# Moving the far attention's softmax up in the order, and six products of the first group from VectorE to GpSimd, in a fused attention and feed-forward kernel

## The chip, the cores and the metric

The kernel runs on one core of a Trainium2 chip. A core has a matrix engine (TensorE, "PE"; its weight loads are listed as "PEld"), a vector engine (VectorE, "DVE"), a scalar engine (ScalarE, "ACT"), a general engine (GpSimd, "POOL") and a queue that issues most transfers (SyncE, "SP"). Each takes its own instructions strictly in the order laid down when the kernel was compiled; semaphores make one wait for another. The metric is the device time of one execution in microseconds (us).

## The reference

For 8 batches of 8 heads, 576 positions and 64 columns the reference adds two attentions and sends the sum through a feed-forward layer. Cut to what matters:

```python
q_d = q.reshape(B, H, Sd, factor, D).mean(axis=3)      # factor 4, so Sd = 144; k_d, v_d alike
out_up = np.repeat(sm_attn(q_d, k_d, v_d), factor, axis=2)
mask = np.abs(pos[:, None] - pos[None, :]) < factor    # 7 neighbours
out_local = softmax(where(mask, scale * q @ k.T, -1e9)) @ v
x = (out_up + out_local).transpose(0, 2, 1, 3).reshape(B * S, H * D)   # 4608 x 512
h = x @ w_in                                           # 512 x 2048
g = s * np.maximum(h, 0) ** 2 + b
return g @ w_out                                       # 2048 x 512
```

The texts call the first attention **far** (all positions, four to a block) and the second **near** (seven neighbours).

## The kernel before

**Feed-forward.** The 4608 rows are cut into 18 token tiles of 256 (t = 0 to 17), the 2048 inner columns into 8 parts (p = 0 to 7). For each pair (t, p) TensorE forms `ph` (L781) from `xh` and `xl`, the high and the low part of x, and the weights `wi`. ACT takes relu, square and the high part `gh` or `gb` (L796 to L798), VectorE the low part `gl` (L803), and TensorE adds the product with `wo` into `po` (L871 to L873). These matmuls stand on TensorE in an order that the program writes out by hand (`products`, L1037): each is tied behind the one before, and `chain_end` is the last one issued so far. A tile needs `xh` and `xl` of its rows; they are cut from x by a cast on ACT (L758) and a subtraction on VectorE (L759).

**Attention.** A batch has 576 rows, that is two and a quarter tiles. Tile 6 (rows 1536 to 1791) is the first that holds rows of batch 3, tile 9 the first of batch 4. Batches 0 to 2 are worked by a long order written out by hand (`PLAN`). Batches 3 to 7 are worked in 10 **groups** (`GROUPS`, `two_pairs`), two to a batch. A group has two **halves** (of near work) and two **units** (of far work), a unit being one pair of heads of a batch. So there are 20 halves and 20 units; groups 0 and 1 are batch 3 with units 0 to 3, and x of a batch is complete when both of its groups have been added to it.

**Near work of a half** (`two_pairs`, L651). For seven offsets POOL multiplies q by shifted k into `pr` (L673; in the first group every second one is VectorE's), VectorE sums each product over the columns (L675). `pr` has two buffers. Then comes a short softmax on VectorE and ACT (L684 to L692), then seven more offsets in which VectorE multiplies v by a weight (L702) and POOL or VectorE adds to `acc` (L703; in the first group always VectorE). The half's data `lqk` has one buffer, so the next half's load is issued when the last product of this half has been formed. At a group's end VectorE transposes `acc` (L713), SP stores it to DRAM (L718) and loads it back in another layout (L723), and POOL adds it to x (L731), which is issued one half later.

**Far work of a unit** (`far_chain`, L556). It is a generator that `two_pairs` calls at every third offset, five steps to a unit:

1. `begin_far`: VectorE sums q and k in blocks of four (L529, L531), ACT spreads q into `dq` (L535).
2. On TensorE the unit before is ended: `up` from its probabilities in `both` (tile `pd`) and the values in `dq` (L547, L549). Right behind it stand this unit's scores `sa` (L578). ACT spreads `up` over x (L552). Then come VectorE's maximum (L589), ACT's scaling of it (L590) and three exponentials with sums (L592).
3. ACT's sum with the small constant (L596), VectorE's reciprocal (L597), ACT's three scalings (L599).
4. Two transposes on VectorE into `ft` (L606), two stores to DRAM (`away`, L610), and seven loads back into `both` in the layout that `up` needs (L615, L621).
5. Nothing.

`far_values` prepares the unit's values on POOL, issued between steps 2 and 3: `vt` and `vq` (L310, L311), then `dq` (L314, L315), which must wait until the `up` of the unit before has read the old ones. The second transpose writes into the same single buffer as `vt`.

**What sets the order.** The framework lays down each engine's order when it compiles the kernel. Among instructions that can go it prefers the one issued earlier in the program. Inside `tc.high_priority()` an instruction is ranked as if it stood at the program's start, so it is preferred to all that is not. L796 to L803 are issued like this, and so are `up` and `sa`, which besides are tied behind `chain_end` on TensorE (`behind`). Steps 3 and 4 and the maximum and exponentials of step 2 are not.

Of the kernel before, what the change touches and what calls it, by code (L numbers as in the profile page):

```python
# [11 lines left out]
F32 = mybir.dt.float32  # L12
# [34 lines left out]
GQ = 48  # L47
NQ = SD // GQ
# [38 lines left out]
def attention_ffn_kernel(ctx, tc, qk, vw_in, vr_in, vdm, qkn, vn, w_in, w_out, s_in, b_in, out):  # L87
    nc = tc.nc
# [3 lines left out]
    def pool(name, bufs, gap=0):  # L92
        if gap:
            ctx.enter_context(tc.tile_pool(name="gap_" + name, bufs=1)).tile(
                [P, gap // 4], F32, name="gap")
        return ctx.enter_context(tc.tile_pool(name=name, bufs=bufs))
# [6 lines left out]
    one = pool("one", 1)  # L103
# [8 lines left out]
    def bank(i, shape, name):  # L112
        return ps.tile(shape, F32, tag=f"k{i}", name=name)
# [442 lines left out]
    def far_chain(units, banks):  # L556

        held = None
        for b, hp in units:
            kd = begin_far(b, hp)  # L560
            yield
            with tc.high_priority(), behind(nc.tensor.engine, chain_end):
                spread = held and end_far(*held, banks)
                with behind(nc.tensor.engine):
                    scores = far_scores(kd, banks)
            if held:
                spread()
            held = b, hp, (yield from far_rest(b, hp, scores))
            yield
        with behind(nc.tensor.engine, chain_end):  # L570
            spread = end_far(*held, banks)
        spread()

    def far_scores(kd, banks):

        sa = banks([2 * GQ, NQ, SD], "sa")
        for i in range(NQ):
            nc.tensor.matmul(sa[:, i], diag[0][1][:, i], kd, start=True, stop=True)  # L578
        return sa

    def far_rest(b, hp, sa):

        tmp = lambda shape, name, tag: one.tile(shape, F32, tag=tag, name=name)
        n = 2 * GQ
        dmx = tmp([P, 2, NQ], "dmx", "dmx")[0:n]
        both = tmp([P, NQ * SD], "pd", "pd")
        pd = both[0:n].rearrange("p (i k) -> p i k", i=NQ)
        dsm = tmp([P, NQ], "dsm", "dsm")[0:n]
        nc.vector.tensor_reduce(dmx[:, 0], sa, AX.X, ALU.max, negate=True)  # L589
        nc.scalar.mul(dmx[:, 1], dmx[:, 0], SCALE / 16)  # L590
        for i in range(NQ):
            nc.scalar.activation(  # L592
                pd[:, i], sa[:, i], AF.Exp, bias=dmx[:, 1, i : i + 1],
                scale=SCALE / 16, accum_out=dsm[:, i : i + 1])
        yield
        nc.scalar.activation(dsm, dsm, AF.Identity, bias=eps[0:n], scale=4.0)  # L596
        nc.vector.reciprocal(dsm, dsm)  # L597
        for i in range(NQ):
            nc.scalar.mul(pd[:, i], pd[:, i], dsm[:, i : i + 1])  # L599
        yield  # L600


        away = {}
        for k0, w, tag in ((0, 3, "ptm"), (KM, 2, "vt")):
            ft = tmp([n, w, n], "ft", tag)
            nc.vector.transpose(  # L606
                ft.rearrange("p w (h i c) -> p w i h c", h=2, i=NQ),
                pd[:, :, k0 : k0 + 32 * w].rearrange("p i (w h c) -> p w i h c", w=w, h=2))
            away[k0] = far_off.tile([n, w, n], F32, name="away")
            nc.sync.dma_start(away[k0], ft)  # L610
        pm = both[0:KM, 0 : 3 * n].rearrange("p (r n) -> p r n", r=3)
        pr = both[:, 3 * n : 3 * SD].rearrange("p (r n) -> p r n", r=3)
        for w in range(3):
            m = min(32, KM - 32 * w)
            nc.sync.dma_start(  # L615
                pm[32 * w : 32 * w + m],
                away[0][:, w].rearrange("(r a) n -> a r n", r=3)[0:m])
        for h in range(2):
            for w in range(2):
                at = 64 * h + 32 * w  # L620
                nc.sync.dma_start(  # L621
                    pr[at : at + 32],
                    away[KM][:, w, GQ * h : GQ * h + GQ].rearrange("(r a) n -> a r n", r=3))
        yield
        return both

    halves = [(b, g, h) for b, g in GROUPS for h in range(2)]
    near_in = {}
# [13 lines left out]
    def load_far(i, parts):  # L642
        if i < len(far_units):
            load_parts(*far_units[i], parts)
# [6 lines left out]
    def two_pairs(b, g, dn):  # L651

        at = GROUPS.index((b, g))
        i = 0

        def far():
            nonlocal i
            if i % 3 == 2:
                next(dn)
            if i == 17:  # L660
                load_far(2 * at + 2, ("qk",))
            i += 1

        acc = None
        st = bank(7, [P, 2, P], "st")
        for h in range(2):
            half = 2 * at + h
            lqk, lv = near_in[half, "lqk"], near_in[half, "lv"]
            ls = take(st[:, h], 0, [P, CH, NO])
            sums = st[:, h, 64 : 64 + CH]  # L670
            for o in range(NO):
                pr = two.tile([P, CH, D], F32, tag="pl", name="pr")
                (nc.vector if at == 0 and o % 2 else nc.gpsimd).tensor_tensor(  # L673
                    pr, lqk[:, 0:CH], lqk[:, CH + o : 2 * CH + o], ALU.mult)
                nc.vector.tensor_reduce(ls[:, :, o], pr, AX.X, ALU.add)  # L675
                if o == NO - 1:
                    load_near(half + 1, "lqk")
                    far_values(half)
                    while late:
                        late.pop()()  # L680
                far()
                yield
            row = lambda t: t.unsqueeze(2).to_broadcast([P, CH, NO])
            nc.vector.tensor_tensor(ls, ls, omask, ALU.add)  # L684
            lr = two.tile([P, 2, CH], F32, tag="lr", name="lr")
            nc.vector.tensor_reduce(lr[:, 0], ls, AX.X, ALU.max)
            nc.vector.tensor_tensor(ls, ls, row(lr[:, 0]), ALU.subtract)
            nc.scalar.activation(ls, ls, AF.Exp, scale=SCALE)
            nc.vector.tensor_reduce(sums, ls, AX.X, ALU.add)
            nc.vector.tensor_scalar(sums, sums, 1e-9, None, ALU.add)  # L690
            nc.vector.reciprocal(lr[:, 1], sums)
            nc.vector.tensor_tensor(ls, ls, row(lr[:, 1]), ALU.mult)  # L692
            far()
            yield
            acc = acc or two.tile([P, CH, 2, D], F32, tag="qk", name="acc")
            for o in range(NO):
                w = ls[:, :, o : o + 1].to_broadcast([P, CH, D])
                if o == 0:
                    nc.vector.tensor_tensor(acc[:, :, h], lv[:, 0:CH], w, ALU.mult)
                else:  # L700
                    pv = two.tile([P, CH, D], F32, tag="pv", name="pv")
                    nc.vector.tensor_tensor(pv, lv[:, o : o + CH], w, ALU.mult)  # L702
                    (nc.vector if at == 0 or o % 3 == 1 else nc.gpsimd).tensor_tensor(  # L703
                        acc[:, :, h], acc[:, :, h], pv, ALU.add)
                if o == NO - 1:
                    load_near(half + 1, "lv")
                far()
                yield
        x = xt[b]
        moved, away = [], []  # L710
        for h in range(2):
            ft = two.tile([P, 2, CH * 32], F32, tag="pv", name="ft")
            nc.vector.transpose(  # L713
                ft.rearrange("p e (i b) -> p e i b", i=CH),
                acc[:, :, h].rearrange("p i (e a) -> p e i a", e=2))
            moved.append(ft)
            away.append(far_off.tile([P, 2, CH * 32], F32, name="away"))
            nc.sync.dma_start(away[h], ft)  # L718
        load_far(2 * at + 3, ("qk",))
        yield  # L720
        for u in range(2):
            for e in range(4):
                nc.sync.dma_start(  # L723
                    moved[u][32 * e : 32 * e + 32],
                    away[e // 2][64 * u : 64 * u + 64, e % 2].rearrange("(r a) n -> a r n", r=2))
        yield

        def add():
            for u in range(2):
                xv = x[:, 2 * g + u].rearrange("p (r b i) -> p r b i", r=2, b=32)  # L730
                nc.gpsimd.tensor_tensor(  # L731
                    xv, moved[u].rearrange("p r (i b) -> p r b i", i=CH), xv, ALU.add)
            complete.update((b, 2 * g + u) for u in range(2))

        late.append(add)
        yield
# [92 lines left out]
    held = {}  # L829
# [149 lines left out]
    at = {"sa": 0, "tp": 0, "up": 0, "tr": 1, "sl0": 1, "sl1": 0, "ol": 1}  # L979
# [225 lines left out]
```

## Time and profile before

| what | value |
|---|---|
| median of 3 runs | 945.68 us (943.19 to 946.14) |
| the profiled execution, its own time | 947.76 us |
| its span, first to last instruction | 946.0 us |
| mean granted TensorE clock | 0.991 |

The profile is of one execution. Its page gives each engine's busy time; the windows give the same for stretches of time, with the granted clock (third number from the end), the share of the DMA engines and GB/s behind the engines. A line of the timeline has the start and the duration in us, the engine, the source line, the operation, the tiles (out<-in) and in brackets how long the engine idled before it and on whom it waited. A line of the waits has the total in us, the number of times and the longest. "SPq" is SP's queue. Matmuls are pipelined, so their spacing, not their listed length, is what one costs.

### The profile page before, as it was taken

How to read it: one execution, taken by the hardware profiler on the slowest of the kernel's cores; microseconds unless marked ns; L12 is line 12 of the kernel's file. 1: busy time of each engine (PE TensorE's matmuls, PEld its weight loads, DVE VectorE, ACT ScalarE, POOL GpSimd, SP SyncE). 2: the span in 40 equal slices, each digit the busy share in tenths (PEclk: the TensorE clock that was granted, in tenths of full speed). 3: DMA queues.
4: the chain of work that ended last, by engine and by line, in shares of the span. 5: the costliest groups of instructions: out<-in, count | busy, mean ns of one | idle time of the engine just before them, and what ended most of it. 6: DMA issues, size and time to landing. Idle time of an engine off the chain costs nothing.

```text
span 946.0 us, 18560 instructions
## 1 busy us (share of the span) xinstructions
PE 907.2 (96%) x7106; PEld 815.8 (86%) x7106; DVE 665.6 (70%) x1148; ACT 462.2 (49%) x1073; POOL 434.7 (46%) x447
## 2 busy tenths in 40 slices
PE   6699999999999997999999999999989999999998
PEld 5588888788888896999988998899889899999997
DVE  9999999854599888878888778777879662111111
ACT  7977774466464352534444444534344433233331
POOL 6401120010324778777877778787887730000000
PEclk9989999999999998999999999999999999999999
DMA  9755413122343445444343526353444220000000
GB/s 322 270 161 195 147 46 119 46 92 71 112 122 95 152 130 157 135 127 133 113 154 115 155 86 174 95 175 113 122 135 131 74 73 1 23 1 24 1 23 23
DMA packets 60505, 105.09 MB, mean 111 GB/s; under 512 B 20480, under 2 KB 34048, under 8 KB 60416
## 3 DMA queue, kind: packets, MB, share of 16 engines
q1 hardware_dynamic: 56096, 96.03, 32.9%
q10 hardware_dynamic: 4320, 7.87, 2.2%
q8 instruction: 56, 0.92, 0.4%
q14 instruction: 33, 0.27, 0.1%
HBM read 84.85 MB, written 19.02 MB: 110 GB/s over the span
## 4 chain that ended last, share of the span: by engine, by line
PE 30%; POOL 15%; DVE 12%; DMA 8%; SPq 3%; issue 3%; ACT 1%; DVEq 0%; POOLq 0%; ACTq 0%
PE ph L781 15%; POOL pr L673 9%; POOL acc L703 5%; PE po L871 5%; PE po L872 5%; PE po L873 5%; DMA lqk<-in_qkn_dram 4%; DVE pv L702 2%; DVE acc L703 2%; DMA tqk<-in_qk_dram 2%; DVE st L675 2%; DMA pd<-away 1%; SPq L723 1%; DMA away<-ft 1%; SPq L621 1%
## 5 line engine op out<-in xcount | busy, mean ns | idle before, releaser
L781 PE MATMUL ph<-xh,wi 128*128 128x256 f32 x2176 | 412.8, 280 | 6.0 <-ACT xh L758 4.7
L781 PEld LDWEIGHTS ph<-xh,wi 128*128 128x128 f32 x2176 | 345.8, 189 | 15.4 <-ACT xh L758 5.2
L781 PE MATMUL ph<-xl,wi 128*128 128x256 f32 x1152 | 320.6, 278 | 0.0
L673 POOL TENSOR_TENSOR pr<-lqk 128x576 f32<-128x576 f32 x134 | 198.2, 1501 | 80.3 <-DMA lqk<-in_qkn_dram 45.3
L781 PEld LDWEIGHTS ph<-xl,wi 128*128 128x128 f32 x1152 | 217.9, 189 | 7.6
L796 ACT ACTIVATE ph<-ph 128x512 f32<-128x512 f32 x144 | 83.8, 582 | 265.3 <-PE ph L781 256.8
L871 PE MATMUL po<-wo,gh 128*128 128x512 f32 x416 | 165.9, 399 | 0.2 <-DVE os L836 0.2
L872 PE MATMUL po<-wo,gh 128*128 128x512 f32 x416 | 163.6, 393 | 0.0
L873 PE MATMUL po<-wo,gl 128*128 128x512 f32 x416 | 162.9, 392 | 0.7 <-DVE gl L803 0.6
L803 DVE TENSOR_TENSOR gl<-ph,gh 128x512 fp32r<-128x512 f32 x104 | 71.0, 682 | 92.9 <-ACT gh L798 92.6
L675 DVE TENSOR_REDUCE st<-pr 128x9 f32<-128x576 f32 x140 | 105.2, 752 | 43.6 <-POOL pr L673 42.5
L703 POOL TENSOR_TENSOR acc<-acc,pv 128x576 f32<-128x576 f32 x72 | 104.6, 1453 | 46.9 <-DVE acc L703 24.2
L314 POOL TENSOR_TENSOR dq<-vt 80x64 f32<-80x64 f32 x58 | 21.1, 377 | 174.4 <-PE up L385 173.0
L702 DVE TENSOR_TENSOR pv<-lv,st 128x576 f32<-128x576 f32 x120 | 87.3, 745 | 18.5 <-POOL acc L703 18.0
L873 PEld LDWEIGHTS po<-wo,gl 128*128 128x128 f32 x416 | 78.3, 188 | 18.6 <-DVE gl L803 1.5
L871 PEld LDWEIGHTS po<-wo,gh 128*128 128x128 f32 x416 | 78.2, 188 | 13.2 <-ACT pd L599 0.4
L872 PEld LDWEIGHTS po<-wo,gh 128*128 128x128 f32 x416 | 78.5, 189 | 11.3 <-issue 0.2
L797 ACT ACTIVATE ph<-ph 128x512 f32<-128x512 f32 x144 | 83.8, 582 | 3.7
L798 ACT CAST gh<-ph 128x512 fp32r<-128x512 f32 x104 | 61.0, 587 | 20.1 <-PE po L872 16.8
L871 PE MATMUL po<-wo,gb 128*128 128x512 f32 x160 | 62.9, 393 | 0.3 <-DVE os L836 0.3
L872 PE MATMUL po<-wo,gb 128*128 128x512 f32 x160 | 62.8, 392 | 0.0
L873 PE MATMUL po<-wo,gb 128*128 128x512 f32 x160 | 62.4, 390 | 0.0
(176 smaller groups left out, 1200.1 us busy)
## 6 DMA issues: line engine op xcount, KB each, us to landing
tqk<-in_qk_dram SPq DMA_DIRECT2D x30, 584.0 KB, 4.0
lqk<-in_qkn_dram SPq DMA_DIRECT2D x20, 768.0 KB, 4.6
lv<-in_vn_dram SPq DMA_DIRECT2D x20, 480.0 KB, 3.5
out_dram<-os ACTq DMA_DIRECT2D x30, 256.0 KB, 3.2
wst<-in_moe_w_in_dram SPq DMA_DIRECT2D x7, 1024.0 KB, 5.9
wst<-in_moe_w_out_dram SPq DMA_DIRECT2D x7, 1024.0 KB, 5.1
away<-ft SPq DMA_DIRECT2D x20, 288.0 KB, 2.3
ft<-away SPq DMA_DIRECT2D x80, 72.0 KB, 2.0
```

The lines of the kernel that those rows point to most:

```text
L673: (nc.vector if at == 0 and o % 2 else nc.gpsimd).tensor_tensor(pr, lqk[:, 0:CH], lqk[:, CH + o : 2 * CH + o], ALU.mult)
L675: nc.vector.tensor_reduce(ls[:, :, o], pr, AX.X, ALU.add)
L702: nc.vector.tensor_tensor(pv, lv[:, o : o + CH], w, ALU.mult)
L703: (nc.vector if at == 0 or o % 3 == 1 else nc.gpsimd).tensor_tensor(acc[:, :, h], acc[:, :, h], pv, ALU.add)
L781: nc.tensor.matmul(ph[:, j], wi[p][:, s, k, f], xk[:, k], start=k == 0 and s == 0 and xk is xh, stop=k == NK - 1 and s == 1)
L796: nc.scalar.activation(ph, ph, AF.Relu)
L797: nc.scalar.activation(ph, ph, AF.Square)
L798: nc.scalar.copy(gh, ph)
L803: nc.vector.tensor_tensor(gl, acc.pop((t, p)), gh.bitcast(F32), ALU.subtract)
L871: nc.tensor.matmul(po[m], gh[:, j, ms], wo[p][:, 0, j], start=first, stop=False)
L872: nc.tensor.matmul(po[m], gh[:, j, ms], wo[p][:, 1, j], start=False, stop=False)
L873: nc.tensor.matmul(po[m], gl[:, j, ms], wo[p][:, 0, j], start=False, stop=last)
```

## The change

The exponentials' function ends with the sum's constant now and is issued right behind `sa` with high priority; the reciprocal, the scalings, the transposes and all nine transfers form a second function, issued with high priority in the next step. So step 2 holds all up to L596, step 3 all the rest, and steps 4 and 5 are empty. The six products of the first group that were VectorE's are POOL's.

```diff
@@ far_chain
             if held:
                 spread()
-            held = b, hp, (yield from far_rest(b, hp, scores))
+            with tc.high_priority():
+                probs = far_probs(scores)
+            held = b, hp, probs[0]
+            yield
+            with tc.high_priority():
+                far_turn(*probs)
+            yield
+            yield
             yield
...
-    def far_rest(b, hp, sa):
+    def far_probs(sa):
...
                 pd[:, i], sa[:, i], AF.Exp, bias=dmx[:, 1, i : i + 1],
                 scale=SCALE / 16, accum_out=dsm[:, i : i + 1])
-        yield
         nc.scalar.activation(dsm, dsm, AF.Identity, bias=eps[0:n], scale=4.0)
+        return both, dsm
+
+    def far_turn(both, dsm):
+
+        tmp = lambda shape, name, tag: one.tile(shape, F32, tag=tag, name=name)
+        n = 2 * GQ
+        pd = both[0:n].rearrange("p (i k) -> p i k", i=NQ)
         nc.vector.reciprocal(dsm, dsm)
         for i in range(NQ):
             nc.scalar.mul(pd[:, i], pd[:, i], dsm[:, i : i + 1])
-        yield
...
-        yield
-        return both
...
@@ two_pairs
-                (nc.vector if at == 0 and o % 2 else nc.gpsimd).tensor_tensor(
+                nc.gpsimd.tensor_tensor(
                     pr, lqk[:, 0:CH], lqk[:, CH + o : 2 * CH + o], ALU.mult)
```

## The prediction

> **What bounds the kernel now.** I read the page first, then the windows, the waits of TensorE, and its timeline around its one long wait.
>
> ```profile
> span 946.0 us, 18560 instructions
> PE 907.2 (96%) x7106; PEld 815.8 (86%) x7106; DVE 665.6 (70%) x1148; ACT 462.2 (49%) x1073; POOL 434.7 (46%) x447
> ...
> 256.00:735.00 479.00, 464.49 (x3056) 422.74 (x3055) 396.98 (x686) 219.19 (x537) 354.03 (x316) 0.99 0.43 131
> ...
> PE up L547 <- DMA pd<-away: 8.6, 9, 1.8
> PE ph L781 <- ACT xh L758: 4.7, 1, 4.7
> PE ph L781 <- DVE gl L803: 1.3, 1, 1.3
> ```
>
> TensorE is the bound, and its work is untouched. From 256 to 735 us, where the changed code runs, it was busy 464.5 of 479.0 us: 14.5 us without a matmul. The waits name them: nine times `up` (L547) stood for the returned probabilities (8.6 us together), once `ph` stood for `xh` (4.7), once for `gl` (1.3).
>
> ```profile
> 367.63 0.39 PE L873 MATMUL po<-wo,gl 128*128 128x512 f32 x1
> 372.76 0.58 PE L781 MATMUL ph<-xh,wi 128*128 128x256 f32 x1 [4.75 <-ACT xh L758]
> 374.97 0.82 PE L547 MATMUL up<-pd,dq 128*128 128x144 f32 x2 [1.63 <-DMA pd<-away]
> ...
> 368.96 3.31 POOL L731 TENSOR_TENSOR x<-ft,x 128x576 f32<-128x576 f32 x2
> 372.31 1.35 ACT L758 CAST xh<-x 128x256 fp32r<-128x256 f32 x2 [1.48 <-POOL x L731]
> ...
> 370.00:372.00 2.00, 0.00 (x0) 0.00 (x0) 1.52 (x8) 0.21 (x1) 2.00 (x2) 0.63 0.96 301
> 372.00:374.00 2.00, 0.58 (x1) 0.29 (x1) 2.00 (x4) 1.35 (x2) 0.44 (x2) 0.50 0.98 253
> 380.00:382.00 2.00, 2.00 (x16) 2.00 (x16) 1.80 (x3) 1.72 (x9) 1.92 (x2) 0.81 0.40 96
> ```
>
> The long wait stands before token tile 6, the first that needs batch 3, and batch 3 comes out of groups 0 and 1. Read upward: TensorE waits for the cast L758, that for the additions L731 on POOL. Behind it the granted clock (third number from the end) is 0.50 until about 380.8 us. TensorE ran in 372.76 to 373.34 and 374.97 to 380.8, 6.4 us at half speed: 3.2 us of work lost. So this place costs 4.75 + 1.63 + 3.2 = 9.6 us.
>
> Later batches are not tight. Batch 4 is complete at 471.19 + 3.51 = 474.70, and tile 9, the first to use it, begins at 520.01:
>
> ```profile
> 471.19 3.51 POOL L731 TENSOR_TENSOR x<-ft,x 128x576 f32<-128x576 f32 x2
> ...
> 520.01 0.28 PE L781 MATMUL ph<-xh,wi 128*128 128x256 f32 x1
> ```
>
> So 45 us of room: from there what TensorE gains at `up` is kept.
>
> **Part 1: six products from VectorE to POOL (group 0).**
>
> ```profile
> L673 DVE TENSOR_TENSOR pr<-lqk 128x576 f32<-128x576 f32 x6 | 5.1, 854 | 1.2 <-DMA lqk<-in_qkn_dram 1.1
> L673 POOL TENSOR_TENSOR pr<-lqk 128x576 f32<-128x576 f32 x134 | 198.2, 1501 | 80.3 <-DMA lqk<-in_qkn_dram 45.3
> ...
> 280.00:300.00 20.00, 19.68 (x126) 17.67 (x125) 19.19 (x35) 8.91 (x23) 6.91 (x6) 1.00 0.48 147
> 320.00:340.00 20.00, 18.69 (x132) 17.14 (x131) 16.71 (x32) 8.95 (x24) 17.02 (x16) 1.00 0.53 167
> ...
> 249.56 1.44 POOL L673 TENSOR_TENSOR pr<-lqk 128x576 f32<-128x576 f32 x1 [7.16 <-DMA lqk<-in_qkn_dram]
> 268.81 1.92 POOL L673 TENSOR_TENSOR pr<-lqk 128x576 f32<-128x576 f32 x1 [4.71 <-DMA lqk<-in_qkn_dram]
> ...
> 264.53 0.72 DVE L675 TENSOR_REDUCE st<-pr 128x9 f32<-128x576 f32 x1
> ```
>
> In group 0 VectorE is the pace: from 280 to 300 us it is busy 19.2 of 20 us, POOL 6.9 (in group 1, from 320 on, 16.7 and 17.0). It loses six products, 5.1 us, and the 1.1 us that one of them stood for `lqk` with other work behind it: at most 6.2 us. POOL gains 6 x 1.50 = 9.0 us, hidden in its idle time unless it becomes the pace: seven products in a row need 7 x 1.44 and the last reduction 0.72, 10.8 us, where the first half took 249.56 to 265.25, 15.7. VectorE would still need 13. POOL's products lengthen beside a VectorE product (1.92 against 1.44 in the last pair of rows); for some three more such, and 0.5 us for far work now ahead of the near work, I take off 1.7. Batch 3 is ready **4.5 us earlier**; ends: 0 if POOL takes the pace, 6.2.
>
> [...]
>
> TensorE comes to tile 6 earlier too: without its wait of 1.09 at 326 us and with about half of the 1.3 for `gl`, 1.8 us. What idles is then 4.75 + 1.8 - 4.5 = 2.0 us; the gain in time is the 4.5.
>
> **The clock.** It fell about 2.5 us into the long idle (0.63 over 370 to 372 is full until 370.5; the last matmul ended at 368.0). A wait of 1.84 did not lower it:
>
> ```profile
> 688.53 0.48 PE L547 MATMUL up<-pd,dq 128*128 128x144 f32 x2 [1.84 <-DMA pd<-away]
> ...
> 680.00:700.00 20.00, 18.16 (x116) 16.27 (x115) 14.85 (x28) 9.17 (x25) 14.84 (x15) 1.00 0.62 181
> ```
>
> 2.0 us is nearer to 1.84 than to 2.5, so I take the **3.2 us** as recovered; ends 0 and 3.2.
>
> **Part 2: the far work early.** For one far unit nothing is added: one maximum, three exponentials, one sum, one reciprocal, three scalings, two transposes and nine DMAs. What moves is their place. The transposes and DMAs are issued one step sooner, all of it goes ahead of near work on VectorE and ACT, and the DMAs ahead of the near ones on SP. Unit 16 shows what that takes away:
>
> ```profile
> 654.65 0.90 PE L578 MATMUL sa<-kd,dq 128*96 128x144 f32 x6
> 665.75 0.72 DVE L606 STREAM_TRANSPOSE ft<-pd 96x288 f32<-96x288 f32 x2
> 671.77 2.24 SPq L718 DMA_DIRECT2D away<-ft  x2
> 675.22 1.81 SPq L610 DMA_DIRECT2D away<-ft  x2
> ```
>
> Scores end at 655.55, transposes at 666.47, but the store waits on SP until 675.22, behind the near stores L718, which wait for the near transposes. The returns follow it, and `up` waits 1.84 us at 688.53 (above). Nearest to undelayed is unit 6:
>
> ```profile
> 395.33 0.90 PE L578 MATMUL sa<-kd,dq 128*96 128x144 f32 x6
> 396.27 0.60 DVE L589 TENSOR_REDUCE dmx<-sa 96x3 f32<-96x432 f32 x1
> 401.01 0.73 DVE L606 STREAM_TRANSPOSE ft<-pd 96x288 f32<-96x288 f32 x2
> ```
>
> 5.5 us from scores to turned. Unit 16 by that: turned at 661.0, stored 14 us sooner; a wait of 1.84 is gone seven times over. Units not held on SP gain less, unit 17 some 4.6 us (turned at 700.35 now, at 690.25 + 5.5 then), and need about 1:
>
> ```profile
> 689.35 0.90 PE L578 MATMUL sa<-kd,dq 128*96 128x144 f32 x6
> 699.63 0.72 DVE L606 STREAM_TRANSPOSE ft<-pd 96x288 f32<-96x288 f32 x2
> 706.78 0.48 PE L547 MATMUL up<-pd,dq 128*128 128x144 f32 x2 [1.01 <-DMA pd<-away]
> ```
>
> The waits of TensorE from 376 to 760 us give the sum, and its 1.63 at 374.97 comes on top:
>
> ```profile
> PE up L547 <- DMA pd<-away: 5.9, 7, 1.8
> ```
>
> I take **1.6 + 5.4** (nine tenths of 5.9); ends 0 and 7.5. The order of `up` on TensorE is held by the chain of products and does not change.
>
> **What it costs.** The second transpose needs `vt`, which POOL's L314 frees; L310 of the next unit then waits for a buffer that comes free sooner. The far returns on SP can stand before the `lqk` load that paces POOL: unit 16's two stores held SP 1.81 us, and in the tight batch four such loads could meet them; I take one meeting in about half of its length, 1.0. Far work on ACT ahead of L796 can delay `gh`; I take 0.5. Together **1.5**, ends 0 and 4 x 1.81 = 7.2.
>
> **Sum.** 4.5 + 3.2 + 1.6 + 5.4 - 1.5 = 13.2 us off. The profiled execution took 947.76 us (946.0 and 1.76 around the span), 2.1 over the median of 945.68; its waits are those of any run, so 934.6 for it and **932.5 us** at the median.
>
> **Rivals.** (a) *Batch 3 is no sooner*: POOL or the serial line of loads paces groups 0 and 1 (for it: from 320 us on POOL, with 17.0 of 20, is ahead of VectorE; against: in group 0, where the products move, it is not). The long wait and the low clock stay; 1.6 + 5.4 - 1.5 = 5.5 off, 940.2.
>
> (b) *SP still holds the even units' stores*, because the near stores keep their place in its line. Then unit 4's 1.63 stays, and later only the odd units' waits go, unit 17's 1.01 and these:
>
> ```profile
> 498.58 0.48 PE L547 MATMUL up<-pd,dq 128*128 128x144 f32 x2 [0.42 <-DMA pd<-away]
> 603.31 0.48 PE L547 MATMUL up<-pd,dq 128*128 128x144 f32 x2 [0.30 <-DMA pd<-away]
> ```
>
> 4.5 + 3.2 + 1.7 - 1.5 = 7.9 off, 937.8. Against: in unit 16 L606 (665.75) stands 6 us before the first near store (671.77), so a store with first place should come first.
>
> (c) *VectorE is held in line, slower*: its reciprocal and transposes, put first, wait for ACT with near work, and `gl`, behind them. Unit 6's chain from the maximum's end (396.9) to the transposes (401.0) would be 4.1 us of idling, in units 0 to 3 16.4 us, all before batch 3 is ready: 16.4 - 4.5 - 1.6 - 5.4 + 1.5 = 6.4 over, 952.1. It decides from 2.5 us per unit on. Against it, the waits of VectorE from 380 to 735 us:
>
> ```profile
> DVE gl L803 <- ACT gh L798: 2.9, 5, 0.9
> DVE dsm L597 <- ACT dsm L596: 0.5, 1, 0.5
> ```
>
> `gl` has first place already, and VectorE stood for it only 2.9 us: the order puts an instruction near the time its input is done.
>
> (d) *It does not do what it says*: the far chain is tied to `vt` and SP's waits and hardly moves, and early far work eats Part 1. About 945.
>
> [...]
>
> **Chances.** Forecast 0.47, (a) 0.20, (b) 0.12, (c) 0.11, (d) 0.10. About 0.3% (2.8 us) is what a measurement of this kernel can tell from no change. Faster: forecast, (a) and (b), less 0.01 for an (a) with a larger cost, 0.78; same 0.11; slower 0.11. The best ends, 6.2 + 3.2 + 1.6 + 5.9, give 928.8, and near transfers freed on SP could add one or two: 927. Upward the range takes in (b), (a) and (d), to 946; (c) stays out.
>
> **What would show it.** Right: no wait of L547 over 0.3 us; L610 within 1 us of L606 in every unit; the wait before tile 6 near 2 us with clock 1.00 behind it; group 0's near transposes (L713) some 4 us sooner than before. Wrong: VectorE waiting at L597 or L606 for ACT or POOL; POOL waiting longer for `lqk`; a new wait of `ph` for `gl`; the wait for `xh` as long as before.

## The result, and the profile after

The change made the kernel slower, by 14.0 us or 1.5%.

| kernel | median | range | ratio to before, 95% interval |
|---|---|---|---|
| before | 945.23 us | 943.19 to 946.14 | |
| after | 959.25 us | 958.44 to 959.65 | 1.0149 (1.0134 to 1.0164) |

The forecast was 932.5 us, the range 927 to 946. The profiled execution of the kernel after took 958.44 us, 0.8 below its median, and that of before 947.76, 2.5 above its own; so the two spans are only 10.7 us apart. From the maximum on, line numbers of the kernel after are some 8 higher than before's: the maximum is L596, the reciprocal L610, the transposes L616, the far stores L620 and returns L625 and L631, POOL's products L681, VectorE's `pv` L710, the near stores L726, the near loads L731, POOL's addition to x L739, the cast L766, `ph` L789, relu L804, `gl` L811.

The kernel after, page and windows (as in the fence of before):

```profile
span 956.7 us, 18552 instructions
...
256.00:735.00 479.00, 456.92 (x2987) 415.36 (x2986) 391.61 (x668) 215.20 (x530) 357.46 (x319) 0.98 0.42 128
```

In the same 479 us TensorE was busy 456.9 us instead of 464.5: it waited 22.1 us instead of 14.5. The waits of 250 to 780 us (total, times, longest) say for what:

```profile
POOL x L739 <- DMA ft<-away: 20.5, 10, 4.0
ACT dq L535 <- DVE qd L529: 12.5, 9, 3.9
DVE pv L710 <- POOL x L739: 7.7, 8, 1.9
...
PE up L547 <- DMA pd<-away: 5.6, 4, 2.6
PE ph L789 <- DVE gl L811: 4.7, 4, 1.9
PE ph L789 <- ACT xh L766: 4.4, 1, 4.4
PE po L879 <- DVE os L844: 2.0, 1, 2.0
PE po L879 <- ACT gh L806: 1.9, 1, 1.9
PE ph L789 <- DVE xl L767: 1.8, 1, 1.8
PE ph L789 <- DVE gb L811: 1.2, 1, 1.2
PE po L879 <- DVE dsm L610: 0.4, 1, 0.4
```

Before, the same stretch had for POOL's addition:

```profile
POOL x L731 <- DMA ft<-away: 6.9, 2, 6.6
```

`up` waits 3.0 us less than before (5.6 against 8.6). In its place TensorE waits for evictions and for one subtraction: for `gl` 4.7 us where it was 1.3, and `os`, `gh`, `xl` and `gb`, 6.9 us together, which were next to nothing. All its waits here come to 22.0 us; before they were 15.1 (the prediction's 8.6, 4.7 and 1.3, and 0.5 for `os`). And POOL's addition to x, which waits for the near loads, stands 20.5 us in ten places where it stood 6.9 in two. That line turned out to be the lead to the cause.

Of the 10.7 us of span, 6.9 are these waits. Most of the rest is the clock, in the next fences: TensorE's timeline after, and the granted clock (third number from the end) in chosen windows.

```profile
336.10 0.47 PE L879 MATMUL po<-wo,gh 128*128 128x512 f32 x1 [1.95 <-ACT gh L806]
370.55 0.48 PE L547 MATMUL up<-pd,dq 128*128 128x144 f32 x2 [2.62 <-DMA pd<-away]
376.76 0.58 PE L789 MATMUL ph<-xh,wi 128*128 128x256 f32 x1 [4.45 <-ACT xh L766]
379.13 0.58 PE L789 MATMUL ph<-xl,wi 128*128 128x256 f32 x1 [1.79 <-DVE xl L767]
...
473.33 0.48 PE L547 MATMUL up<-pd,dq 128*128 128x144 f32 x2 [2.32 <-DMA pd<-away]
493.76 0.39 PE L789 MATMUL ph<-xh,wi 128*128 128x256 f32 x1 [1.95 <-DVE gl L811]
596.16 0.47 PE L879 MATMUL po<-wo,gb 128*128 128x512 f32 x1 [2.05 <-DVE os L844]
```

```profile
372.00:374.00 2.00, 0.31 (x3) 0.02 (x1) 1.51 (x6) 1.21 (x7) 2.00 (x3) 0.52 0.93 185
382.00:384.00 2.00, 2.00 (x18) 2.00 (x17) 0.75 (x1) 0.00 (x0) 2.00 (x3) 0.92 0.26 42
474.00:474.50 0.50, 0.50 (x7) 0.50 (x6) 0.43 (x3) 0.47 (x2) 0.00 (x0) 0.98 0.74 168
477.50:478.00 0.50, 0.50 (x3) 0.39 (x2) 0.50 (x2) 0.00 (x0) 0.50 (x2) 0.61 1.02 430
494.50:495.00 0.50, 0.50 (x4) 0.43 (x3) 0.50 (x1) 0.00 (x0) 0.50 (x1) 0.96 0.30 74
597.00:597.50 0.50, 0.50 (x6) 0.50 (x5) 0.50 (x2) 0.00 (x0) 0.50 (x1) 0.86 0.01 4
```

The mean clock was 0.50 over 474.50 to 477.50 and 1.00 over 478 to 480. Between these two speeds, 0.98 over 474.00 to 474.50 puts the fall at 474.48, and 0.61 over 477.50 to 478.00 the rise at 477.89. So after a wait of 2.32 us TensorE ran 3.41 us at half speed and lost 1.7. The waits of 1.95 and 2.05 us are followed by a fall as well (494.96, 597.36), as long as the first: the means of 0.81 over 498 to 499 and 0.86 over 600.50 to 601.50 put the rises at 498.38 and 600.78, so 1.7 us each. From 372.08 to 382.32, at tile 6 (0.50 over 374 to 382), some 4.0 us of matmuls ran at half speed: 2.0 lost. That is 7.1 us, 3.9 more than the 3.2 of before. With 6.9 it makes 10.8. But 0.8 of the 10.7 us were there before the changed code ran: the groups' first `lqk` load was issued at 246.15 us, before at 245.36. So the account is about 0.9 us too large, and that its sum comes so near to 10.7 is in part luck.

### The profile page after: what moved, and what is told of

It reads as the page before. It is cut to its first block, busy times and chain, and to the rows that moved or that the text cites. A ratio compares the mean times of both kernels' runs of the same rounds, so it can differ in the third digit from the quotient of the medians.

```text
span 956.7 us, 18552 instructions
## 1 busy us (share of the span) xinstructions
PE 908.2 (95%) x7106; PEld 816.0 (85%) x7106; DVE 664.1 (69%) x1142; ACT 461.6 (48%) x1073; POOL 444.1 (46%) x453
## 4 chain that ended last, share of the span: by engine, by line
PE 61%; DVE 13%; POOL 9%; DMA 8%; SPq 3%; issue 3%; ACT 2%; DVEq 0%; POOLq 0%; ACTq 0%
PE ph L789 28%; PE po L879 10%; PE po L880 9%; PE po L881 9%; POOL pr L681 5%; DMA tqk<-in_qk_dram 2%; POOL acc L711 2%; DMA lqk<-in_qkn_dram 2%; DVE pv L710 1%; SPq L631 1%; PE ol L481 1%; DVE es L274 1%; SPq L731 1%; DMA wst<-in_moe_w_in_dram 1%; DVE gl L811 1%
## 5 line engine op out<-in xcount | busy, mean ns | idle before, releaser
L789 PE MATMUL ph<-xh,wi 128*128 128x256 f32 x2176 | 413.4, 281 | 10.3 <-DVE gl L811 4.7
L789 PEld LDWEIGHTS ph<-xh,wi 128*128 128x128 f32 x2176 | 347.1, 190 | 21.0 <-DVE gl L811 6.7
L789 PE MATMUL ph<-xl,wi 128*128 128x256 f32 x1152 | 322.2, 280 | 2.9 <-DVE xl L767 1.8
L681 POOL TENSOR_TENSOR pr<-lqk 128x576 f32<-128x576 f32 x140 | 204.6, 1487 | 71.1 <-DMA lqk<-in_qkn_dram 50.8
L789 PEld LDWEIGHTS ph<-xl,wi 128*128 128x128 f32 x1152 | 218.8, 190 | 10.6 <-DVE xl L767 2.1
L804 ACT ACTIVATE ph<-ph 128x512 f32<-128x512 f32 x144 | 83.8, 582 | 257.5 <-PE ph L789 246.5
L811 DVE TENSOR_TENSOR gl<-ph,gh 128x512 fp32r<-128x512 f32 x104 | 70.9, 682 | 88.6 <-ACT gh L806 88.3
L710 DVE TENSOR_TENSOR pv<-lv,st 128x576 f32<-128x576 f32 x120 | 87.6, 745 | 29.5 <-POOL acc L711 21.3
L314 POOL TENSOR_TENSOR dq<-vt 80x64 f32<-80x64 f32 x58 | 23.4, 415 | 174.9 <-PE up L385 173.4
```

Source lines behind the costliest of these rows:

```text
L681: nc.gpsimd.tensor_tensor(pr, lqk[:, 0:CH], lqk[:, CH + o : 2 * CH + o], ALU.mult)
L789: nc.tensor.matmul(ph[:, j], wi[p][:, s, k, f], xk[:, k], start=k == 0 and s == 0 and xk is xh, stop=k == NK - 1 and s == 1)
L804: nc.scalar.activation(ph, ph, AF.Relu)
L811: nc.vector.tensor_tensor(gl, acc.pop((t, p)), gh.bitcast(F32), ALU.subtract)
```

## The experiments

Three theories stood at the start. L: the loss comes from the high priority of the far work, chiefly from the maximum and the exponentials, put ahead of evictions on ScalarE. P: it comes from the six products on POOL. S: it comes from the steps that were moved. Ratios are to the kernel before, run beside them on the same chip; its medians there were 943.18, 945.99, 945.36 and 946.92 us in the four groups in which the experiments ran.

### Which part of the change: e1, e2, e3, e4

**e1**, the kernel before with the six products on POOL and nothing else:

```diff
-                (nc.vector if at == 0 and o % 2 else nc.gpsimd).tensor_tensor(
+                nc.gpsimd.tensor_tensor(
```

> The kernel before with the six products of group 0 on POOL and nothing else. Theory L (held in line: the far work put first on ACT and VectorE delays the evictions of ph, and TensorE idles for gl, gh and os): this has none of that, so the products alone are worth what the prediction gave them, about 4 us less than before, some 941 us. Theory P (the products on POOL are the loss): slower than before by most of the 14 us, 952 to 959.

Measured: 942.94 us, ratio 0.9994 (0.9979 to 1.0009). **e2**, the kernel after with this one line put back:

> The changed kernel with the six products of group 0 back on VectorE. Theory L: the whole loss stays and the gain of the products is missing, 959 to 964 us. Theory P: the loss is gone, 945 or below.

Measured: 956.13 us, ratio 1.0129 (1.0102 to 1.0157). P falls: the products change nothing that can be told, in either kernel. Both texts miss their numbers under L (some 941, and 959 to 964), since both counted on a gain of some 4 us from the products. **e3**, the kernel after without both priorities, so only the steps are moved (and the products are on POOL):

```diff
-            with tc.high_priority():
-                probs = far_probs(scores)
+            probs = far_probs(scores)
...
-            with tc.high_priority():
-                far_turn(*probs)
+            far_turn(*probs)
```

> The changed kernel without high priority on the far work: the steps are where the change put them (turning one step sooner), in plain program order. Theory L: the evictions keep their place ahead, so the loss is gone: 938 to 945 us, the mean time from the last ph matmul to the end of gl back near 4.9 us (before 4.88, changed 5.58). Rival S (the loss comes from the steps being sooner, through SP's queue and the shared buffers): still 953 to 959.

Measured: 941.98 us, ratio 0.9990 (0.9969 to 1.0010). S falls too; the whole loss is the priority. **e4** leaves it on the second function alone:

```diff
-            with tc.high_priority():
-                probs = far_probs(scores)
+            probs = far_probs(scores)
```

> The changed kernel with high priority on the turning alone (reciprocal, scalings, transposes, transfers); maximum, exponentials and sums in plain order. Theory L, if ACT's wait for the maximum (28.0 us in the changed kernel against 10.2 before) and the exponentials are the main part: most of the loss is gone, 943 to 949 us. If the turning is the main part: 953 to 959.

Measured: 958.62 us, ratio 1.0157 (1.0129 to 1.0185). So L was right in the priority and wrong in the place: it is the turning, not the maximum and the exponentials.

### Which part of the turning: e5, e6, e7, and the kernel before again

**e5** has the priority on the first function alone. Its text on record says that its products are on VectorE; they are on POOL, as in e3, e6, e7 and e9.

> The steps moved as in the change, the products on VectorE as before; high priority on the maximum and the exponentials alone, none on the scalings, the turning and its transfers. If the whole loss hangs on the turning's priority: within 0.3% of the kernel before (940 to 946 us beside 943.2). If the first half carries a part of it (an exponential put ahead of an eviction on ScalarE): 947 to 953.

Measured: 944.03 us, ratio 0.9978 (0.9963 to 0.9992). **e6** gives it to the nine transfers alone, **e7** to the six computing instructions of the second function alone:

```diff
 e6: e3, and
+            with tc.high_priority():
                 nc.sync.dma_start(away[k0], ft)
...
+        with tc.high_priority():
             for w in range(3):
...
 e7: e3, and
+        with tc.high_priority():
             nc.vector.reciprocal(dsm, dsm)
...
+            with tc.high_priority():
                 nc.vector.transpose(
```

> As the kernel without priority, but the turning's nine transfers alone (two stores, seven returns, all on SP) have high priority; reciprocal, scalings and transposes keep the plain one. Theory SP: the far transfers stand ahead of the near pairs' loads of the turned values on SP, POOL's add then stands in line for those, VectorE and ScalarE after it, and the evictions come late: 954 to 960. Theory compute: the scalings and transposes put to the front of ScalarE and VectorE hold the evictions, and the transfers are harmless: 940 to 946.

> The other half: reciprocal, three scalings and two transposes of a unit with high priority, its nine transfers without. Theory SP: 940 to 946. Theory compute: 954 to 960. If both halves lose (each reorders every queue): both at 948 to 956.

Measured: e6 960.36 us, ratio 1.0153 (1.0131 to 1.0174); e7 944.89 us, ratio 0.9988 (0.9970 to 1.0006). The nine transfers are the whole loss, and the computing with first place costs nothing that can be told. The kernel before, profiled a second time:

> The kernel before, unchanged, for a second profile: the waits that are the same in both profiles belong to the kernel, those that differ to one execution. Expected 941 to 946, a wait of 4 to 5 us before tile 6 in both, and the lengths of the waits of the far output products within 1.5 us of the first profile's.

Measured: 947.00 us, ratio 0.9999 (0.9976 to 1.0022). Its TensorE waited 4.8 us before tile 6 (4.7 in the first profile) and 8.3 for `pd` in 7 places (8.6 in 9): they are not an accident of the first profile. Its time is 1 us over the 946 that its text allowed.

How the transfers do it is to be read in one group of e6 (batch 4's second, units 8 and 9), in the timelines of SP, POOL, VectorE, ScalarE and TensorE. Near loads are L733, far returns L627 and L633, POOL's addition L741.

```profile
463.90 1.65 SPq L728 DMA_DIRECT2D away<-ft  x2
466.62 0.85 SPq L733 DMA_DIRECT2D ft<-away  x2
467.83 2.31 SPq L627 DMA_DIRECT2D pd<-away  x3
470.25 1.77 SPq L633 DMA_DIRECT2D pd<-away  x4
472.07 3.00 SPq L733 DMA_DIRECT2D ft<-away  x6
...
474.74 1.74 POOL L741 TENSOR_TENSOR x<-ft,x 128x576 f32<-128x576 f32 x1 [2.94 <-DMA ft<-away]
...
480.36 0.75 DVE L712 TENSOR_TENSOR pv<-lv,st 128x576 f32<-128x576 f32 x1 [1.91 <-POOL x L741]
482.30 3.69 DVE L769 TENSOR_TENSOR xl<-x,xh 128x1024 fp32r<-128x1024 f32 x1
485.91 0.74 DVE L529 TENSOR_REDUCE qd<-tqk 128x144 f32<-128x576 f32 x1
...
486.68 0.64 ACT L535 COPY dq<-qd 64x144 f32<-64x144 f32 x2 [3.85 <-DVE qd L529]
488.36 0.57 ACT L806 ACTIVATE ph<-ph 128x512 f32<-128x512 f32 x1
...
491.39 0.68 DVE L813 TENSOR_TENSOR gl<-ph,gh 128x512 fp32r<-128x512 f32 x1
...
492.12 0.38 PE L791 MATMUL ph<-xh,wi 128*128 128x256 f32 x1 [1.78 <-DVE gl L813]
```

Read downward. SP issues two of the eight near loads, then the seven far returns, and only from 472.07 on the other six near loads. POOL has reached its addition at 471.8, where it stands 2.94 us for the first half of them. Its second addition stands behind 2.1 us of work on `dq` (L315, L314) and ends at 480.33. The `ft` tiles lie in the two buffers that `pv` uses, so VectorE's `pv` waits for that addition; the subtraction `xl` and `qd` stand in line behind it. ScalarE has reached `dq` and waits 3.85 us for `qd`, and behind it in ScalarE's line stand the relus of two products. So `gl` ends only at 492.07, and TensorE has waited 1.78 us. The returns are out 8.1 us after the near stores' start (472.02 from 463.90).

### Is it the order of near loads and far returns: e8, e9, r1

**e8** is the whole kernel after, with the near group's own ten transfers at high priority as well, which puts its loads ahead of the far returns again. **e9** is the kernel after with the seven returns of a unit plain:

```diff
 e8
+            with tc.high_priority():
                 nc.sync.dma_start(away[h], ft)
...
+        with tc.high_priority():
             for u in range(2):
                 for e in range(4):
                     nc.sync.dma_start(
                         moved[u][32 * e : 32 * e + 32],
 e9
             with tc.high_priority():
-                far_turn(*probs)
+                returns = far_turn(*probs)
+            returns()
```

> The kernel after, whole, and beside it high priority on the near pairs' own two stores and eight loads of turned values, which puts these loads ahead of the unit's seven far returns on SP again, where the kernel without priority has them. The far returns of the other units (those with no near transfers beside them) still stand ahead of a load of lv. Theory near loads (the loss comes from near loads of turned values standing behind seven far returns): 940 to 946. Theory lv and lqk (the loss comes from the near inputs' loads that the far transfers push back in the other units): 952 to 959. Theory any order (the priority changes every queue, and that is the loss): 952 to 959.

> The kernel after, but the seven returns of each unit without high priority; the scalings, the transposes and the two stores keep it. Near loads: 940 to 946, since the near loads stand ahead of the returns again. Theory lv and lqk: 940 to 946 too, since the returns are the longer part there. Theory stores (a far store with first place waits on SP for its transpose and holds what is behind it): 952 to 959.

Measured: e8 948.64 us, ratio 1.0029 (1.0012 to 1.0046); e9 941.10 us, ratio 0.9964 (0.9946 to 0.9982). The same group in e9, SP's and POOL's timelines (near loads L736, far returns L628 and L634, addition L744):

```profile
461.96 1.64 SPq L731 DMA_DIRECT2D away<-ft  x2
464.68 3.67 SPq L736 DMA_DIRECT2D ft<-away  x8
468.46 1.31 SPq L628 DMA_DIRECT2D pd<-away  x3
...
469.95 3.44 POOL L744 TENSOR_TENSOR x<-ft,x 128x576 f32<-128x576 f32 x2
```

Its waits from 250 to 780 us:

```profile
POOL x L744 <- DMA ft<-away: 7.7, 2, 6.8
PE ph L794 <- ACT xh L771: 5.2, 1, 5.2
PE up L547 <- DMA pd<-away: 5.0, 5, 1.6
PE po L884 <- ACT pd L613: 0.3, 1, 0.3
```

All eight near loads are out 6.4 us after the near stores' start, where e6 took 11.2. The returns are out at 472.26, after 10.3 us: the priority bought them 2.2 us and cost the near loads 4.8. POOL's two additions run without a wait there, and the work on `dq` stands behind both of them. How much of e6's delay is the loads' own, and how much this other order on POOL, was not separated. From 250 to 780 us not one wait for an eviction is left. Seven instructions per unit, returned to their place, give back the whole loss. e8 comes down from 1.0149 to 1.0029, by the other way to the same order. So the theories of lv and lqk and of any order, which put e8 at 952 to 959, fall, and with e9 falls that of the stores. e8 misses its own 940 to 946 by 2.6 us. In its profile `up` of unit 4 stands ahead of tile 6's first product on TensorE and waits for its returns, which are behind eight near loads now:

```profile
374.37 0.82 PE L547 MATMUL up<-pd,dq 128*128 128x144 f32 x2 [7.09 <-DMA pd<-away]
```

So the long wait has changed its name there. Whether that is all of the remainder was not tried.

Of the experiments so far only e5 (0.9978) and e9 (0.9964) have an interval wholly below 1, and e9 is the furthest ahead of the kernel before. **r1** is e9 once more, in more rounds:

> The kernel after with the seven returns of each unit plain, a second time and in more rounds, to see how far it is ahead of the kernel before. If the gain of the waits of the far output products is real (5.0 us left of 8.6, and none of the waits for the products' evictions): ratio 0.995 to 0.998. If the first comparison was a lucky draw: 0.998 to 1.001.

Measured: 943.08 us beside 946.92, ratio 0.9958 (0.9941 to 0.9974): about 0.4% faster than before. The reason that its text gives is not borne out: its `up` waits 7.1 us for `pd` (7 places), not 5.0, so they vary from one execution to the next; waits for evictions are absent again. Which part of the change brings the 0.4% was not settled.

### A try at the wait before tile 6: e11

```diff
 e5, and
-                nc.gpsimd.tensor_tensor(
+                (nc.vector if at == 1 and u == 1 else nc.gpsimd).tensor_tensor(
                     xv, moved[u].rearrange("p r (i b) -> p r b i", i=CH), xv, ALU.add)
```

> As the kernel with priority on the maximum and the exponentials alone (six products on POOL, steps moved, the turning plain; 944.0 beside 946.0 before), and group 1's second addition of the turned values into x on VectorE instead of POOL, beside the first one. The two additions end batch 3 one after the other (3.3 us on POOL); side by side they end some 1.4 us sooner, so the wait before tile 6 falls from 5.3 to about 4 us: 940.5 to 943, ratio 0.994 to 0.998. If the second load is what ends last, or VectorE is busy there, no change: 0.997 to 0.999.

Measured: 945.06 us, ratio 0.9997 (0.9980 to 1.0014). The wait before tile 6 was 4.5 us where e5's profile has 5.3; no gain in time that can be told. In the profile, waits for `gl` and `gb` that e5 does not have, 2.2 us together, stand against the 0.8. The rest of that wait stays open.

## Why the prediction was wrong, point by point

**What bounds the kernel** held: TensorE, and its waits and clock account for the result.

**Part 1** was mis-sized. What rival (a) foresaw came about, a long wait and a low clock that stay, but not for its reason: POOL did not take the pace, VectorE kept it. Near transposes in e1, and before (duration min, median, max; first and last start, groups 0 and 1):

```profile
L713 DVE STREAM_TRANSPOSE ft<-acc x4: 758/760/768, 307.5 to 360.5; 128x576 f32<-128x576 f32 x4
```

```profile
L713 DVE STREAM_TRANSPOSE ft<-acc x4: 760/760/762, 309.8 to 362.1; 128x576 f32<-128x576 f32 x4
```

Group 0 ended 2.3 us sooner, not 4.5, group 1 1.6. Where the 4.5 failed is in group 0's second half; POOL's timeline in e1:

```profile
266.71 2.83 POOL L673 TENSOR_TENSOR pr<-lqk 128x576 f32<-128x576 f32 x2 [4.32 <-DVE st L692]
...
281.18 2.48 POOL L673 TENSOR_TENSOR pr<-lqk 128x576 f32<-128x576 f32 x1 [5.79 <-DVE st L675]
```

It begins 2.1 us before the 268.81 of the kernel before, which is the first half's gain; then POOL stands 5.79 us, because VectorE, with its own work, has not summed the products that fill the two buffers. So the second half's products gained almost nothing. And at group 1's end:

```profile
367.92 3.31 POOL L731 TENSOR_TENSOR x<-ft,x 128x576 f32<-128x576 f32 x2
...
371.72 0.58 PE L781 MATMUL ph<-xh,wi 128*128 128x256 f32 x1 [4.86 <-ACT xh L758]
```

The additions began 1.04 us sooner (367.92 for 368.96), and tile 6 as much, but TensorE was there sooner too, so its wait stayed 4.86. Where the six products stood did not matter here: ratio 0.9994 with them on POOL.

**The clock** was not recovered, since the wait stayed; and the assumption that a wait of 2.0 us is safe, the author's estimate from 1.84 and 2.5 us in one execution, fell with the three waits shown above. A fall followed 2.32, 1.95 and 2.05 us of waiting here, while none followed 1.95 before 336.10 in the same execution and 1.84 before 688.53 in the kernel before.

**Part 2** gained less than its 7.0 us. `up` waits 3.0 us less after (3.6 in e9, 1.5 in r1, which are the same kernel, so 3.0 is little more than what differs between executions), but the far chain itself hardly got shorter. Unit 16 after (scores, maximum, second function's transposes, far stores, last near loads):

```profile
667.98 0.90 PE L585 MATMUL sa<-kd,dq 128*96 128x144 f32 x6
...
671.32 0.60 DVE L596 TENSOR_REDUCE dmx<-sa 96x3 f32<-96x432 f32 x1
677.83 0.72 DVE L616 STREAM_TRANSPOSE ft<-pd 96x288 f32<-96x288 f32 x2
...
678.64 0.84 SPq L620 DMA_DIRECT2D away<-ft  x2
684.22 1.37 SPq L731 DMA_DIRECT2D ft<-away  x3
```

From scores to turned it took 9.7 us where 5.5 were forecast and it was 10.9 before. The maximum, with first place, still began 2.4 us after the scores. First place in the program is not first place in time; why the order laid it so late was not tried. The stores went out at once there, as forecast, and the last three near loads at 684.22, behind the far returns: the price. In the even units from 2 to 14 the second store stood 4 to 17 us on SP as before, which is rival (b)'s case.

**What it costs, 1.5 us, is the step that failed.** It looked for the far returns' harm at the `lqk` load, in four places, at half of 1.81 us. The harm does not show there: from 250 to 780 us POOL's waits for `lqk` come to 43.2 us in e6 and 50.8 after, which have the whole loss, to 49.7 in e9, which has none, and to 45.3 before. The returns met another transfer of the same queue, the near group's loads, and held them for 4.2 us in the group shown (467.83 to 472.02 in e6). And the harm is not that length: it went through POOL, VectorE and ScalarE into the evictions and from there into the clock. The ratios of after and e9, 1.0149 and 0.9964, put the seven returns at 0.0185, some 17.5 us of 945, where the forecast had 1.5 for all costs. The upper end of 7.2 for the costs was too low, for the same reason. The gains are the smaller error: e9, without that cost, is 3.4 us (0.36% of 945) faster than before, where 14.7 were forecast; 3.4 less 17.5 gives the 14 us of loss.

**Rival (c)** had the right side and VectorE standing in line, but not the cause: its reciprocal and transposes with first place cost nothing that can be told (e7). VectorE stood for POOL's addition, 7.7 us.

## What to carry to other kernels

A transfer put first in a queue can get ahead of others that the queue still holds (in e6 the seven returns, ahead of six near loads for 4.2 us): list the others there, and for each the engine that stands in line for it, before pricing it at its own issue time. Here what makes a result (the transposes and stores) could have first place without loss (e9). Leave what only fetches it, early and in many pieces, behind those that someone waits for now. A wait for an eviction on a nearly full TensorE (busy 456.9 of 479.0 us) may cost twice: once itself, and once by the clock after it (after, 1.95 us before 493.76 and then 1.7).

## What was not expected of the hardware

The clock fell after the wait, with TensorE running again: the wait before 473.33 was over 1.15 us when the half speed began, and the 3.41 us of it fell on full work. The wait of 1.95 us before 493.76 so cost 3.7, nearly twice itself.

The length of a wait alone does not decide this. The 1.95 us before 336.10 were as long as the 1.95 before 493.76, and no fall followed them: the clock was 1.00 from 330 to 370 us. In e6 a wait of 1.78 us before 492.12 was followed by a fall at about 492.64 (the mean clock was 1.00 over 488 to 492 and 0.58 over 492 to 496 us), while 560 to 640 us, where TensorE stood 2.01 us in all (busy 77.99 of 80.00), shows none, at 1.00. After the 1.84 us of the kernel before there was none either (1.00 from 680 to 700 us). What sets these waits apart was not shown, and no run was made to test it.
